# Decoding attention on one core: q spread two tiles ahead, and eight rows of the last V tile added beside the sum over groups

## Chip, cores, metric

One core of a Trainium2 chip. The metric is the device time of one launch in microseconds. The changed kernel and the kernel before are run in turn on the same chip.

## The reference

```python
B, H, Sq, Skv, Dh = 8, 32, 1, 4096, 128          # bfloat16
scores = einsum('bhqd,bhkd->bhqk', q, k) * Dh ** -0.5
out = einsum('bhqk,bhkd->bhqd', softmax(scores), v)
```

There is one query for each of the 256 heads. K and V are 268 MB each and are read once.

## The kernel before

Heads are worked in 32 tiles of 8. A tile of K or V is 8.4 MB: 128 partitions (16 per head) with 256 rows of 128 numbers each. For each tile the vector engine multiplies K by q and folds it, the tensor engine sums over the head's width, the scalar engine takes the exponentials `w`, and the tensor engine multiplies them with V.

```python
def q_prep(t):                       # spreads the q of 8 heads over 128 partitions
    ... matmul (L164); activation -> qg (L168); matmul (L170); activation -> qb (L172)

cuts = { ...
    ("v", NT - 1): [C // 2, C // 4, C // 8, C // 16, C // 32, LAST, LAST],   # C = 256, LAST = 4
}

def scores_of(t, u):
    if u == 0:
        scs[t] = sc_pool.tile([P, C], F32, name="sc", tag="sc")      # two buffers
    made = nc.vector.tensor_reduce(out=scs[t][:, ...], in_=sums.pop((t, u))[:], ...)   # L217

def values_of(t, lo, hi):            # four rows of V in a matmul; four column groups of the array
    end = C if t < NT - 1 else C - LAST
    group = [0 if t == NT - 1 and C // 2 <= c0 < C // 2 + 3 * C // 16 else c0 // CB % TG
             for c0 in range(0, end, CB)]
    ... matmul into avs[t][group j]                                   # L316

def result_of(t):                    # [cut]
    if t == NT - 1:
        for i in range(LAST):        # the last rows go straight into the result
            nc.tensor.matmul(ops[n][:], lhsT=w_last[:, i, :],
                             rhs=loads["v", t][:, C - LAST + i, :], ...)      # L354
    for m in range(CB):              # the sum over groups, from its copy
        nc.tensor.matmul(ops[n][:], lhsT=pick[...], rhs=comb[0:e, m, :], ...)  # L360

# main (cut)
    q_prep(0)
    for t in range(NT):
        product(t, 0, Q); sum_over_d(t, 0); ...
        if t + 1 < NT: q_prep(t + 1)
        ...
    values_of(NT - 1, 0, C // 2); norm_of(NQ - 1); recip_of(NQ - 1)
    values_of(NT - 1, C // 2, C - LAST)
    copy_of(NT - 1)                  # scalar engine: av -> comb, L344
    result_of(NT - 1); finish_of(NQ - 1); store_of(NQ - 1)
```

## Time and profile before

| | kernel before |
|---|---|
| timed runs | 1253.0, 1253.07, 1253.38 us |
| the profiled run | 1253.7 us, span 1251.9 us |
| HBM read | 536.94 MB, 429 GB/s over the span |
| DMA queue of K, V and q | 99.3% of 16 engines |
| vector, tensor, scalar engine busy | 83%, 61%, 14% |

The queue that carries K and V takes 99.3% of the DMA engines' time, so the end is set by when the last bytes of V land and by what stands behind them. The prediction below reads that tail.

The queues of the page, with packets, MB and share of 16 engines, show also the transfers that bring the instructions:

```profile
q1 hardware_dynamic: 11216, 536.94, 99.3%
q8 instruction: 14, 0.23, 0.1%
q14 instruction: 11, 0.09, 0.0%
```

They are small, 16 KB (q8) each, and take 0.93 to 1.10 us (q8) each in the trace, but the page counts their time as a share of the same 16 engines.

### The profile page before, as it was taken

Reading aid. Unit: us, or ns where it says so; the run is one execution under the profiler, and the core shown is the slowest. Engines: PE = TensorE matmul, PEld = TensorE weight load, DVE = VectorE, ACT = ScalarE, POOL = GpSimd, SP = SyncE. Lnnn points to the kernel's source line nnn. Section 1 sums busy time; section 2 is a strip of 40 time slices with the busy share of each in tenths; the row PEclk is TensorE's granted clock in tenths of the full one; section 3 lists DMA queues with packets and bytes.
Section 4 is the critical chain, followed back from the end, with each engine's and each line's share of the span. In section 5 each row is a group of like instructions: output and inputs, shape, how many; then the busy total and the mean of one; then the engine's idle time right before and its main releaser. Section 6 shows DMA issues by size and latency. Waiting matters only on the chain. (4 is left out here: it accounts for less than half of the span.)

```text
span 1251.9 us, 11042 instructions
## 1 busy us (share of the span) xinstructions
PE 767.1 (61%) x3075; PEld 286.0 (23%) x3075; DVE 1036.0 (83%) x586; ACT 170.6 (14%) x625; POOL 3.3 (0%) x18
## 2 busy tenths in 40 slices
PE   2465467755577555775557755577655676557856
PEld 0122122221222112222212221122211222212212
DVE  7887988888988889888798888987889888898792
ACT  0111011111011110111101111011110111101111
POOL 0000000000000000000000000000000000000000
PEclk8677788777887777887788877788777887779867
DMA  9999999999999999999999999999999999999997
GB/s 404 436 436 434 436 433 432 436 436 434 425 430 430 436 433 436 429 434 430 436 436 434 436 434 432 436 432 430 431 436 434 436 426 436 427 428 429 428 437 317
DMA packets 11577, 537.33 MB, mean 429 GB/s; under 512 B 1824, under 2 KB 2080, under 8 KB 2336
## 3 DMA queue, kind: packets, MB, share of 16 engines
q1 hardware_dynamic: 11216, 536.94, 99.3%
q8 instruction: 14, 0.23, 0.1%
q10 hardware_dynamic: 336, 0.07, 0.0%
q14 instruction: 11, 0.09, 0.0%
HBM read 536.94 MB, written 0.07 MB: 429 GB/s over the span
## 5 line engine op out<-in xcount | busy, mean ns | idle before, releaser
L185 DVE TENSOR_TENSOR kt<-kt,qb 128x8192 bf16<-128x8192 bf16 x128 | 565.3, 4416 | 127.2 <-DMA kt<-in_k_dram 98.9
L205 PE MATMUL ps<-kt,ident 128*128 128x512 bf16 x800 | 262.6, 479 | 434.3 <-DVE kt L193 368.3
L288 PE MATMUL av<-vt,w 128*32 x1740 | 424.5, 394 | 5.5
L188 DVE TENSOR_TENSOR kt<-kt 128x4096 bf16<-128x4096 bf16 x128 | 293.4, 2292 | 4.4
L288 PEld LDWEIGHTS av<-vt,w 128*32 x1740 | 171.9, 99 | 263.8 <-issue 124.9
L205 PEld LDWEIGHTS <-ident 128*128 128x128 bf16 x800 | 86.1, 112 | 597.2 <-issue 549.7
L249 ACT ACTIVATE w<-sc,bias 128x256 bf16<-128x256 f32 x256 | 126.3, 494 | 667.1 <-DVE bias L240 667.1
L217 DVE TENSOR_REDUCE sc<-ps 128x64 f32<-128x512 f32 x128 | 87.8, 686 | 56.6 <-PE ps L205 56.6
L193 DVE TENSOR_TENSOR kt<-kt 128x2048 bf16<-128x2048 bf16 x56 | 68.6, 1225 | 1.9
L344 ACT ACTIVATE comb<-av 32x512 bf16<-32x512 f32 (+1 forms) x32 | 18.7, 585 | 324.5 <-PEq L278 314.0
L274 PE MATMUL av<-vt,w 128*32 128x512 bf16 x116 | 47.1, 499 | 14.7 <-issue 13.2
L249 ACT ACTIVATION_READ_ACCUMULATOR w<-sc,bias 128x1 f32 x256 | 47.7, 186 | 0.0
L274 PEld LDWEIGHTS av<-vt,w 128*32 128x32 bf16 x116 | 6.9, 100 | 55.3 <-issue 55.3
L168 ACT ACTIVATE qg<-qh 8x128 bf16<-8x128 f32 x32 | 8.5, 266 | 76.5 <-PE qh L164 76.5
L316 PE MATMUL av<-vt,w 128*32 128x512 bf16 x191 | 16.4, 428 | 2.0 <-DMA vt<-in_v_dram 2.0
L360 PE MATMUL op<-comb,pick 32*16 32x128 bf16 (+1 forms) x128 | 12.3, 215 | 5.8 <-ACT comb L344 5.8
L229 DVE TENSOR_REDUCE pmax<-sc 128x1 f32<-128x256 f32 x32 | 13.5, 420 | 1.1
L170 PE MATMUL qp<-qg,heads 8*128 8x128 bf16 x32 | 6.9, 214 | 11.4 <-ACT qg L168 11.4
L164 PE MATMUL qh<-q_all,ident 128*8 128x128 bf16 x32 | 7.2, 224 | 8.4 <-DMA q_all<-in_q_dram 8.4
L172 ACT ACTIVATE qb<-qp 128x128 bf16<-128x128 f32 x32 | 8.9, 277 | 9.6 <-PE qp L170 9.6
L360 PEld LDWEIGHTS <-pick 32*16 32x16 bf16 (+1 forms) x128 | 6.8, 84 | 13.1 <-issue 12.7
L316 PEld LDWEIGHTS <-w 128*32 128x32 bf16 x191 | 6.8, 105 | 11.0 <-issue 7.2
(29 smaller groups left out, 46.7 us busy)
## 6 DMA issues: line engine op xcount, KB each, us to landing
kt<-in_k_dram SPq DMA_DIRECT2D x6, 4096.0 KB, 24.6
kt<-in_k_dram SPq DMA_DIRECT2D x4, 2048.0 KB, 13.9
vt<-in_v_dram SPq DMA_DIRECT2D x1, 4096.0 KB, 36.2
vt<-in_v_dram SPq DMA_DIRECT2D x1, 2048.0 KB, 40.8
vt<-in_v_dram SPq DMA_DIRECT2D x1, 1024.0 KB, 42.8
vt<-in_v_dram SPq DMA_DIRECT2D x1, 512.0 KB, 43.6
vt<-in_v_dram SPq DMA_DIRECT2D x31, 25.6
kt<-in_k_dram SPq DMA_DIRECT2D x28, 28.1
```

Source lines behind the costliest of these rows:

```text
L185: nc.vector.tensor_tensor(out=part, in0=part, in1=qb[:].to_broadcast([P, MC, D]), op=ALU.mult)
L188: nc.vector.tensor_tensor(out=part[:, :, 0 : D // 2], in0=part[:, :, 0 : D // 2], in1=part[:, :, D // 2 : D], op=ALU.add,)
L193: nc.vector.tensor_tensor(out=part[:, :, 0 : D // 4], in0=part[:, :, 0 : D // 4], in1=part[:, :, D // 4 : D // 2], op=ALU.add,)
L205: nc.tensor.matmul(ps[:], lhsT=ident[:], rhs=kt[:, u * UC : (u + 1) * UC, s * DS : (s + 1) * DS], start=(s == 0), stop=(s == n - 1),)
L217: made = nc.vector.tensor_reduce(out=scs[t][:, u * UC : (u + 1) * UC], in_=sums.pop((t, u))[:], axis=AX.X, op=ALU.add)
L229: nc.vector.tensor_reduce(out=pmax[:], in_=sc[:], axis=AX.X, op=ALU.max)
L249: nc.scalar.activation(out=w[:, :, g, :], in_=sc_g, func=ACT.Exp, bias=bias[:, g : g + 1], scale=scale, accum_out=esum[:, t % R, g : g + 1],)
L274: pe.matmul(av, lhsT=wf[:, i * nw : (i + 1) * nw], rhs=vf[:, i * nv : (i + 1) * nv], **how)
L288: pe.matmul(av, lhsT=wf[:, bass.ds(ow + i * nw, nw)], rhs=vf[:, bass.ds(ov + i * nv, nv)], start=False, stop=False,)
L316: nc.tensor.matmul(avs[t][j * AG : (j + 1) * AG, :], lhsT=w[:, i, :, :], rhs=vt[:, c0 : c0 + CB, :], start=(i < TG), stop=(j not in group[ ...
L344: nc.scalar.activation(out=comb[0:n, :, :], in_=av[0:n, :, :], func=ACT.Copy)
L360: nc.tensor.matmul(ops[n][:], lhsT=pick[0:e, m, r, :], rhs=comb[0:e, m, :], start=(r == 0 and m == 0), stop=(r == R - 1 and m == CB - 1),)
```

## The change

The intent as it reads: have each q ready earlier, and take one more matmul out of the chain behind the last landing, by adding eight rows and not four straight into the result.

```diff
-LAST = 4
+LAST = 8
-    q_pool = ... bufs=2
+    q_pool = ... bufs=3
-        ("v", NT - 1): [C // 2, C // 4, C // 8, C // 16, C // 32, LAST, LAST],
+        ("v", NT - 1): [C // 2, C // 4, C // 8, C // 16, C // 32, LAST // 2, LAST // 2],
-            nc.gpsimd.tensor_copy(... w_last ..., in_=w[:, (C - LAST) // CB, :, :])
+            for i in range(LAST // CB):
+                nc.gpsimd.tensor_copy(... w_last part i ..., in_=w[:, (C - LAST) // CB + i, :, :])
         q_prep(0)
+        q_prep(1)
         for t in range(NT):
             ...
-            if t + 1 < NT:
-                q_prep(t + 1)
+            if t + 2 < NT:
+                q_prep(t + 2)
```

The pieces of V keep their sizes (4 and 4 at the end).

## The prediction

Its sum: 0.0 for q and 0.0 to -0.05 us for the eight rows, on 1253.07, came to 1253.0. One more instruction block: that added instructions could need one, and the 1254 if one comes, are estimates. "Such blocks" in it are the 16 KB transfers of q8, and "cold" is half clock, at which the long matmuls of the first profile start 0.427 us apart and not 0.216.

> **What bounds the kernel now.** I read the summary page first, its slices of the span. The DMA row is at 9 in every slice but the last, while the vector engine stays at 7 to 9 and the tensor engine at 4 to 7.

> ```profile
> DVE  7887988888988889888798888987889888898792
> PEclk8677788777887777887788877788777887779867
> DMA  9999999999999999999999999999999999999997
> GB/s 404 436 436 434 436 433 432 436 436 434 425 430 430 436 433 436 429 434 430 436 436 434 436 434 432 436 432 430 431 436 434 436 426 436 427 428 429 428 437 317
> ```

> Added up over 20 us stretches, the DMA packets in the trace keep all 16 engines busy (mean 16.0) from about 5 us to 1240 us. So K and V set the pace: 536.94 MB at 433 GB/s, the usual rate of the slices, is 1240 us, and the measured span is 1251.9 us. The 12 us between are the ramp at the start, the uneven finish of the engines and the work behind the last bytes. Only the last of these has a part of the change in it.

> Next the timeline of the vector engine at the start of a tile, because the page blames several of its waits on the scalar engine, and the spread of q is made there.

> ```profile
> 81.04 4.43 DVE L185 TENSOR_TENSOR kt<-kt,qb 128x8192 bf16<-128x8192 bf16 x1 [3.73 <-DMA kt<-in_k_dram]
> 160.01 4.43 DVE L185 TENSOR_TENSOR kt<-kt,qb 128x8192 bf16<-128x8192 bf16 x1 [4.32 <-ACT stage L369]
> ```

> The second looks like a wait for the scalar engine. But the K tile landed at 159.82, and in the first case at 80.95: both products start 0.1 to 0.2 us after the landing. The same holds at every tile from 81 to 1091 us where this product stood waiting over 1 us. The name in brackets is a guess; the wait is for K.

> Last the chain that ended last, and the timeline of the tensor and scalar engines under it.

> ```profile
> 1201.69 40.81 DMA vt<-in_v_dram
> 1242.50 0.04 issue
> 1242.54 5.49 PE av L316 x29
> ...
> 1248.11 0.60 ACT comb L344
> 1248.72 0.04 issue
> 1248.76 0.40 PE op L360 x4
> 1249.15 0.02 issue
> 1249.18 0.36 ACT stage L369
> ```

> ```profile
> 1242.54 5.43 PE L316 MATMUL av<-vt,w 128*32 128x512 bf16 x31 [2.01 <-DMA vt<-in_v_dram]
> 1247.81 0.39 PE L354 MATMUL op<-vt,w_last 128*16 128x128 bf16 x4
> 1248.76 0.38 PE L360 MATMUL op<-comb,pick 128*16 128x128 bf16 x4 [0.56 <-ACT comb L344]
> ```

> V's last tile comes in seven pieces of 128, 64, 32, 16, 8, 4 and 4 rows. The chain names one landing only: that of the 64 rows at 1242.50. Then the tensor engine runs without a gap through its 31 matmuls to about 1248.0. The later pieces landed, by the transfers' own records, at 1244.99, 1246.21, 1246.86 (8 rows), 1247.20 (4 rows) and 1247.51 (last 4).

> What keeps it busy is column group 0. The kernel puts the first twelve matmuls of this stretch there, one after the other, and every fourth of the others: 17 in all. In the single records they start at 1242.54 and then 0.427 us apart, up to about 1245.87 (eight intervals with the first a little shorter), then 0.216 us apart; the last, of row 240, starts at 1247.592 and ends at 1247.97. The last matmul in program order, of rows 248 to 251, sits in group 2, started at 1247.24 just behind its landing, and is done before that. It is the one that the change removes.

> [...] the granted clock goes from half to full at 1245.81, one window after the boundary at 1242.40. [...] the best slices show 434 to 437[...]. [...] the page of the kernel before shows 14 such blocks (0.23 MB on q8). In the landings one engine is 1.4 us behind the next at the end, and it was 0.02 us behind before the first such block at 97 us. So added instructions could cost DMA time, if they need another block.

> **The change part by part.**

> *q two tiles ahead.* 32 spreads before and 32 after. Each is two matmuls (224 and 214 ns), two scalar activations (266 and 277 ns) and the handshakes: at 19.91 to 21.06 us it takes 1.15 us. In the order of instructions the second spread moves to the head, right behind the first; each later one takes the old place of the spread before it, and the last body that had one, at tile 30, has none. At the head the vector engine starts at 9.61 on the first q. The second spread comes behind that on both engines, about 9.6 to 10.8, where the tensor engine stands idle until 16.41 and the scalar engine until 20.22. Cost 0. In the loop no product waits for q, so gain 0. At tile 30 the tensor engine has about 1.1 us less to do, but the weights of tile 31 are ready at 1236.8, and from 1240.5 to 1242.54 the engine only waits for V: up to 2 us of such gain vanish there. The third buffers of qg and qb are 256 bytes per partition each. Sum: 0.

> *Eight rows straight into the result.* Removed: one 128x512 matmul, the one in group 2 that was not the last to end. Group 0's chain is the same 17 matmuls from the same landing. What may go is its completion: the semaphore that frees the scalar copy counts at 1247.993 and then 1248.027, so an estimate of 0.03 us. Added: four 128x128 matmuls, eight in place of four. The first started at 1247.81, 0.216 us behind the last long one, and they follow at 0.056 us: starts to 1248.20, end at 1248.20 + 0.22 = 1248.42. The copy of the sum runs from 1248.11 to 1248.71 beside them, and the four L360 matmuls that need it start at 1248.76. So 0.34 us of slack is left: cost 0. Their second four need the landing of 1247.51, past by then. The second POOL copy of weights is another 0.32 us behind 1237.39, ten us before its use. The larger memset (128x128 instead of 128x64; one of that size takes 0.19 us) lies at 2 us, before anything needs it.

> The pieces of V keep their sizes, so the transfers are the same. Sum of both: 0.0 to -0.05 us on 1253.07, so 1253.0.

> **The rivals.**

> *The landing of rows 248 to 251 was the real last wait.* Then the copy could start one landing earlier, 1247.20 - 1246.86 = 0.34 us: 1252.7. For it: it seems to be what the change is for. Against it: 1247.20 + 0.04 + 0.38 = 1247.62 is 0.35 us ahead of group 0's end. I give it one chance in five, in runs where the window of the clock falls better.

> *q held up the vector engine.* The rows that name the scalar engine before L185 add up to 17.4 + 4.2 us. If they were real, and if the vector engine set the end, the time would be about 1232. The landings contradict the first and the saturated DMA the second. One in a hundred.

> *The eight short matmuls outlast the copy.* [...]

> *The window of the clock falls elsewhere.* [...] In the profiled run it began 0.14 us before the landing, near the best case. At worst all 17 matmuls of group 0 are cold: nine more times 0.211 = 1.9 us, 1255. That is chance and not the change, and the three runs of before lie within 0.38 us.

> *One more instruction block.* The change adds three pairs of weight load and matmul to the tensor engine, six rows in 3030, and one instruction to POOL. [...] one DMA engine gets up to 1.1 us more (a block's time in the trace): 1254. Some 3 chances in 100.

> **Range and chances.** Point 1253.0. Downward the rival of the landing (0.34) and a spread like that of before (0.4) give 1252.3; upward the same spread and a window somewhat worse give 1253.8. A change of 2% is 25 us; that needs something in the DMA stream, which the change does not touch. Faster 0.01, same 0.985, slower 0.005.

> **What would show it.** Right: DMA at 9 throughout, the last landings near 1247.5, the copy of the sum about 0.6 us behind them, the eight short matmuls done before it, L185 still starting 0.1 us behind each K landing. The first step fails if the copy starts over 0.2 us earlier relative to the landing of the 64 rows; the second if the L360 matmuls start later than the copy's end; the part on q if L185 starts earlier relative to K's landing. The whole is wrong if the landings themselves shift, by instruction blocks on another engine or by a DMA queue that ran dry.

## The result, and the profile after

The changed kernel took 1252.65, 1252.72, 1252.76 and 1252.91 us, median 1252.74, against 1253.04 for the kernel before in four runs. The ratio is 0.9997 (95% interval 0.998 to 1.0014): no change at the 2% level. Ratios here are the mean time of one kernel's runs over that of the other's of the same rounds, so not quite the ratio of the medians. The time lies inside the predicted range. The profile shows another tail than the one predicted.

Slices of the span in the kernel after, in tenths for the granted clock and the DMA share:

```profile
PEclk9977788777887778877778777788777887778867
DMA  9999999999999999999999999999999999999997
```

The stream is as full as before. Its chain that ended last, in the same columns as before:

```profile
1204.53 41.99 DMA vt<-in_v_dram
1246.53 0.04 issue
1246.57 0.41 PE av L317 x2
...
1247.06 0.61 ACT comb L345
1247.66 0.04 issue
1247.71 0.40 PE op L361 x4
1248.10 0.02 issue
1248.13 0.36 ACT stage L370
```

And its tensor engine in the timeline:

```profile
1242.24 3.40 PE L317 MATMUL av<-vt,w 128*32 128x512 bf16 x24 [1.09 <-DMA vt<-in_v_dram]
1245.97 0.40 PE L317 MATMUL av<-vt,w 128*32 128x512 bf16 x4 [0.33 <-DMA vt<-in_v_dram]
1246.57 0.39 PE L317 MATMUL av<-vt,w 128*32 128x512 bf16 x2 [0.20 <-DMA vt<-in_v_dram]
1246.89 0.70 PE L355 MATMUL op<-vt,w_last 128*16 128x128 bf16 x8
```

In the kernel before the chain hung on the landing of the 64 rows at 1242.50 and was tensor work from there on. Here the tensor engine waits three times, and the chain hangs on the landing of the 8-row piece at 1246.53: two matmuls, the copy, the sum, the store. Its clock was full (granted 1.0 from 1233.70 to 1250.77 us; column group 0 advances by 0.216 us from the start), so group 0 was done early. The copy starts at 1247.06 and not at 1248.11. The two profiled runs, of 1253.7 and 1252.65 us, differ by as much as these two copies, 1.05 us. But the medians of the timed runs differ by only 0.3 us. So either the kernel before is not usually as its first profile shows it, or something was lost elsewhere.

The DVE (vector engine) timeline has one more difference. The first product of tile 29, in the kernel after and in the kernel before:

```profile
1091.92 4.43 DVE L185 TENSOR_TENSOR kt<-kt,qb 128x8192 bf16<-128x8192 bf16 x1 [4.25 <-DMA kt<-in_k_dram]
```

```profile
1091.27 4.43 DVE L185 TENSOR_TENSOR kt<-kt,qb 128x8192 bf16<-128x8192 bf16 x1 [4.25 <-DMA kt<-in_k_dram]
```

It is 0.65 us later. From there on the vector engine never waits for K again, and the last weights are later too: the last exponentials start at 1237.65 in place of 1236.34.

### The profile page after: what moved, and what is told of

It is laid out like the page before. It is cut to its first block, busy times and chain, and to the rows that moved or that the text cites. A ratio compares the mean times of both kernels' runs of the same rounds, so it can differ in the third digit from the quotient of the medians.

```text
span 1250.9 us, 11080 instructions
## 1 busy us (share of the span) xinstructions
PE 770.4 (62%) x3078; PEld 289.4 (23%) x3078; DVE 1036.1 (83%) x586; ACT 170.7 (14%) x625; POOL 3.5 (0%) x19
## 2 busy tenths in 40 slices
DMA  9999999999999999999999999999999999999997
## 3 DMA queue, kind: packets, MB, share of 16 engines
q1 hardware_dynamic: 11216, 536.94, 99.4%
HBM read 536.94 MB, written 0.07 MB: 429 GB/s over the span
## 5 line engine op out<-in xcount | busy, mean ns | idle before, releaser
L185 DVE TENSOR_TENSOR kt<-kt,qb 128x8192 bf16<-128x8192 bf16 x128 | 565.3, 4416 | 127.9 <-DMA kt<-in_k_dram 103.5
L205 PE MATMUL ps<-kt,ident 128*128 128x512 bf16 x800 | 265.3, 483 | 432.4 <-DVE kt L193 366.8
L217 DVE TENSOR_REDUCE sc<-ps 128x64 f32<-128x512 f32 x128 | 87.8, 686 | 57.3 <-PE ps L205 57.3
```

The costliest lines, as they stand in the source:

```text
L185: nc.vector.tensor_tensor(out=part, in0=part, in1=qb[:].to_broadcast([P, MC, D]), op=ALU.mult)
L205: nc.tensor.matmul(ps[:], lhsT=ident[:], rhs=kt[:, u * UC : (u + 1) * UC, s * DS : (s + 1) * DS], start=(s == 0), stop=(s == n - 1),)
L217: made = nc.vector.tensor_reduce(out=scs[t][:, u * UC : (u + 1) * UC], in_=sums.pop((t, u))[:], axis=AX.X, op=ALU.add)
```

## The experiments

"Slow tail" below means a time above 1253.3 us. This cut was set by hand: six of the 36 runs of the kernel before lie between 1253.26 and 1253.38, it is the same for kernels whose fast tails differ, and the tail itself was seen only in the profiled runs. The theories: **A**, in most runs the clock is full in the tail and the last wait is the landing of the piece ahead of the last one; **B**, group 0 on the half clock sets the end, as predicted; **C**, the gain is q's; **D** and its sharper forms **E** and **F** say that q acts on how often the clock is halved.

### The kernel before, unchanged

> The kernel before, unchanged: how far two builds of one thing differ, and whether its tail always looks as in the first profile (first matmul of the last 31 followed by others 0.427 us apart, no wait for the later pieces of V, copy of the sum at 1248.1). Theory A (in most runs the clock is full there and the last wait is for the landing of rows 248 to 251; the first profile, at 1253.7 the slowest of its four, caught a half clock): 1253.0 to 1253.1, and this profile, if it is near 1253.0, shows the matmuls 0.216 us apart and a wait for V just before the copy. Theory B (group 0's chain on the half clock sets the end in every run, as predicted): the same time, and the profile looks like the first.

Measured: 1252.98, 1253.03, 1253.04, 1253.35, 1253.58. The nine runs of the shared control beside it went from 1253.0 to 1253.9, three of them above 1253.3. Its profile is of the run of 1252.98:

```profile
1242.21 3.40 PE L316 MATMUL av<-vt,w 128*32 128x512 bf16 x24 [2.17 <-DMA vt<-in_v_dram]
1245.93 0.40 PE L316 MATMUL av<-vt,w 128*32 128x512 bf16 x4 [0.32 <-DMA vt<-in_v_dram]
1246.58 0.72 PE L316 MATMUL av<-vt,w 128*32 128x512 bf16 x3 [0.25 <-DMA vt<-in_v_dram]
1247.24 0.38 PE L354 MATMUL op<-vt,w_last 128*16 128x128 bf16 x4
1248.04 0.38 PE L360 MATMUL op<-comb,pick 128*16 128x128 bf16 x4 [0.42 <-ACT comb L344]
```

That is theory A's tail: full clock (granted 1.00 from 1236 to 1248 us), waits for each piece. The third group here holds three matmuls where the kernel after has two. The third is of rows 248 to 251, which landed at 1246.88 against 1246.54 for the 8-row piece, and the copy starts at 1247.39. The difference, 0.34 us, is what the change removes. One kernel has two tails. The profile that the prediction read was of a slow one.

### q alone

```diff
-LAST = 8
+LAST = 4          # and with it the old cuts and copy; q stays two tiles ahead
```

> Only q two tiles ahead. Theory A: 0.0 (ratio 1.000, within 0.1 us of the kernel before). Rival C (the 0.3 us come from q: less work of the tensor engine at tile 30, or another clock in the tail by it): -0.3 us.

Measured: 1252.98, 1253.03, 1253.04, 1253.15, 1253.49; ratio 0.9999. Its fast tail is that of the kernel before to 0.1 us. C as stated falls: q takes nothing from the fast tail. One run of the five, 1253.49, is above the cut.

### Eight rows alone

```diff
-        q_prep(1)
-            if t + 2 < NT:
-                q_prep(t + 2)
+            if t + 1 < NT:
+                q_prep(t + 1)
```

> Only the eight rows. Theory A: the copy waits for the 8-row piece in place of the 4-row piece behind it, 0.3 us earlier: -0.3 us against the kernel before (1252.7). Theory B: 0.0 to -0.05. Rival C: 0.0.

Measured: 1252.65, 1252.74, 1253.48, 1253.51, 1253.63. Two runs are at A's 1252.7, three at B's time. The profile is of 1253.63. Timeline of the tensor engine, and busy time by stretches (the two numbers before the last are the granted clock and the DMA share):

```profile
1242.42 5.52 PE L317 MATMUL av<-vt,w 128*32 128x512 bf16 x30 [2.17 <-DMA vt<-in_v_dram]
1247.77 0.61 PE L355 MATMUL op<-vt,w_last 128*16 128x128 bf16 x8
1248.69 0.38 PE L361 MATMUL op<-comb,pick 128*16 128x128 bf16 x4 [0.31 <-ACT comb L345]
```

```profile
1242.00:1244.00 2.00, 1.58 (x7) 0.69 (x7) 0.00 (x0) 0.00 (x0) 0.00 (x0) 0.86 0.89 347
1244.00:1246.00 2.00, 2.00 (x12) 0.70 (x11) 0.00 (x0) 0.00 (x0) 0.00 (x0) 0.50 0.36 133
```

The clock was halved at 1243.46, behind an idle stretch of 2.17 us, and came back at 1246.87. The 30 matmuls then run without a wait to 1247.9, past every landing that they need (1246.74 at the latest), and taking one matmul out of group 2 gains nothing: B holds in this tail. So the eight rows are worth 0.35 us in the fast tail (1252.70 against 1253.05, medians of the runs below 1253.3) and nothing to speak of in the slow one. But three of the five runs are slow, and none of the four of the whole change was: something else in it may prevent that.

### The kernel before with the clock held up

```diff
+    def fill(n):                       # nobody reads it
+        ps = ps_s.tile([P, UC, DS], F32, name="ps", tag="ps")
+        for i in range(n):
+            nc.tensor.matmul(ps[:], lhsT=ident[:], rhs=loads["k", NT - 1][:, 0:UC, 0:DS], ...)
                 values_of(t - 1, 0, C)
+                if t == NT - 1: fill(10)
 ...
         recip_of(NQ - 1)
+        fill(8)
         values_of(NT - 1, C // 2, C - LAST)
```

> The kernel before with 18 matmuls that nobody reads (10 behind the last matmuls of tile 30, 8 ahead of the wait for the 64 rows), so that the clock is full in the tail whatever its window. Theory A: as the kernel before, within 0.1 us (1253.0), and the profile shows the wait for the 4-row piece, about 0.03 us after its landing, then 0.38 us of matmul, then the copy. Theory B: the half clock costs 0.4 us or more in every run, so this is 0.4 us faster than the kernel before.

Measured: 1252.99 to 1253.29, median 1253.22, none slow. In its profile the first 24 of the last matmuls take 3.40 us, as at full clock in `before_again`. The copy starts at 1247.51, behind the landing of the 4-row piece at 1247.00, as A has it. The median is 0.17 us above the fast runs without the unread matmuls (1253.05), a little more than the 0.1 us that A allowed. B's 0.4 us of gain is not there. No run is above the cut of 1253.3, though three of the five are within 0.1 us of it.

### The changed kernel again

> The changed kernel again. So far its four runs all had the fast tail (1252.65 to 1252.91), the eight rows alone only two of five (1252.65 and 1252.74, the others 1253.48 to 1253.63), and q alone four of five. Theory D (spreading q earlier delays the last weights by a microsecond, which shortens the idle time of the tensor engine before the 64 rows, and so the half clock comes less often): at most one of five above 1253.3. Rival (the window's chance alone): one to three of five above 1253.3.

Measured: 1252.57 to 1252.82, none slow; with the first four runs, none of nine. Of the nine controls beside it five were slow. The kernel before was slow in 16 of 36 runs, with a mean of 1253.34; the changed kernel has a mean of 1252.71. Theory D's count came true, its reason did not: in this run's profile the half clock was there, from 1238.81 to 1242.22, and it ended as the 64 rows began (1242.16).

### The changed kernel with the clock held up

The edit is the same `fill`.

> The changed kernel with the same 18 unread matmuls. Theory A: no run above 1253.3, and 0.33 us faster than the kernel before with the unread matmuls (whose median was 1253.22): 1252.7 to 1252.9. Its profile shows the copy behind the landing of the 8-row piece. Theory B is out by the profiles of the first four.

Measured: 1252.65 to 1253.1, median 1252.70, none slow, ratio 0.9995. The same 24 matmuls take 3.41 us. The copy (1247.12) follows the landing of the 8-row piece (1246.59). Against the kernel before with the same edit this is 0.5 us by the medians, of two different calls; 0.33 was expected, and the copies in the two profiles are 0.39 us apart.

### Eight rows alone with the clock held up

> Eight rows, q one tile ahead, and the 18 unread matmuls that keep the tensor engine's clock up. Theory E (q's only worth is that its tail meets the half clock less often): no run above 1253.3, median within 0.15 us of the changed kernel with the same unread matmuls (1252.70). Rival (q is worth something on its own, or harms): off by more than that.

Measured: 1252.66 to 1252.86, median 1252.83, none slow; the 24 matmuls take 3.40 us. This is 0.13 us from the changed kernel with the clock held, within what was stated. So with the clock held, moving q is worth about nothing. Without, none of the nine runs with q moved was slow, and three of the five with the eight rows alone.

### Why moving q changes the clock

The traces suggest a link. The vector engine's instructions at L217, in the kernel after, by count and times in ns:

```profile
L217 DVE TENSOR_REDUCE sc<-ps x128: 682/684/693, 22.9 to 1232.2; 128x64 f32<-128x512 f32 x128
L217 DVEq EVENT_SEMAPHORE  x30: 21/21/21, 94.1 to 1211.7; - x30
```

The second row is absent in the kernel before. There the vector engine's wait for q of this tile also told it that the exponentials ahead of that q on the scalar engine had been read from `sc`, whose buffer it was about to write again. With q spread a tile earlier the wait for it comes before those exponentials, and the scheduler adds a wait of its own, 30 here and one at the reciprocal. They take 21 ns each, and the engine's idle time just ahead of L217's work is 57.3 us in all, against 56.6 before. But they are 31 more instructions, and the q14 instruction block that came at 1095.5 us comes at 1032.3 (the last one is then that of 1067.6, which stays in its place). In all four profiles with q two tiles ahead one DMA engine is then 1.3 to 1.7 us behind the next when the K tile of tile 29 lands (1091.74 to 1091.85); in the eight with q one tile ahead and nothing else added to the vector engine it is 0.4 to 0.8 us behind, and the landing is at 1090.83 to 1091.27. This K tile was issued at 1062.8 to 1063.3 in all of them, so it did not start later. That the moved block is what lays the engine behind is argued and not isolated: the block itself takes only 0.32 us. Beside it stands what the first block of q8 (0.93 us long, at 97.5 us) came with: in the first profile one engine was 0.02 us behind the next at the landing of 80.95 us and 1.34 us at that of 101.73; in the kernel after, 0.21 and 1.25 us. The next two runs try the two ends of this.

```diff
 def scores_of(t, u):                   # the eight rows alone, with 31 more vector instructions
+        if u == 0 and t > 0:
+            nc.vector.memset(pad[:], 0.0)        # one element
```

> Eight rows, q one tile ahead, and 31 vector memsets of one element, one for each tile but the first: as many added vector instructions as the 31 waits that moving q brought. Theory F (the added instructions bring the vector engine's last instruction block from 1095 to 1032 us, that lays one DMA engine behind by about 1 us when the K tile of 1091 lands, the last weights come later, the gap ahead of the 64 rows shrinks to 1 us, and the clock stays full): block at 1032, that K landing at 1091.7 to 1091.9 in place of 1090.8 to 1091.2, at most one of five above 1253.3. Rival (it is the place of q's matmuls and activations): block and landing as the eight rows alone, or three of five above 1253.3 in spite of them.

Measured: the block at 1017.9 (earlier than expected), the K landing at 1091.95, all five runs 1252.66 to 1252.80. The times are as F has it: q is where it was in the kernel before, and they are those of the changed kernel. But the clock did not stay full, as F said. It was half from 1240.40 to 1243.81, into the 30 matmuls that start with the 64 rows:

```profile
1239.33 2.57 PE L320 MATMUL av<-vt,w 128*32 128x512 bf16 x29
1242.35 4.76 PE L320 MATMUL av<-vt,w 128*32 128x512 bf16 x30 [0.42 <-DMA vt<-in_v_dram]
```

It came back early enough for these matmuls to catch up: the copy starts at 1247.21, 0.54 us behind the landing of the 8-row piece (1246.67), against 0.53 us in the kernel after.

```diff
 def weights_of(t):                     # the eight rows alone, with the vector engine held up
+        if t == NT - 2:
+            for i in range(2):
+                late = small.tile([P, 1], F32, name="late", tag="late")
+                nc.vector.tensor_reduce(out=late[:], in_=sc[:], axis=AX.X, op=ALU.max)
```

> Eight rows, q one tile ahead, and the vector engine held up by two reductions (0.84 us) nobody reads, in tile 30, behind every wait for K. Theory F: block at 1095 and K landing at 1091.0 as before, but the last weights 0.8 us later, the gap ahead of the 64 rows about 1.2 us in place of 2.0 to 2.2, and at most one of five above 1253.3; so work added to the vector engine makes the kernel's median faster, 1252.7. Rival: two to four of five above 1253.3, as the eight rows alone (three of five).

Measured: the block at 1095.3, the K landing at 1090.90, all five runs 1252.63 to 1253.01. Its tensor engine:

```profile
1238.60 3.52 PE L321 MATMUL av<-vt,w 128*32 128x512 bf16 x29
1242.31 3.40 PE L321 MATMUL av<-vt,w 128*32 128x512 bf16 x24 [0.16 <-DMA vt<-in_v_dram]
```

The gap ahead of the 64 rows is 0.16 us here and not 2.17, or the 1.2 that F expected, and the last exponentials start at 1237.02, 0.27 us later than with the eight rows alone (1236.75) and not 0.8. In this run the clock was half from 1238.7 to 1242.1, but the work on the first 128 rows then filled that time, and it was full again from 1242.1. So a delay of under a microsecond, on an engine that is not the bound, goes with the eight rows paying in all five runs. Together: with late weights (q alone, the changed kernel, and these two) 1 slow run of 24; with early ones and no unread matmuls (kernel before, eight rows, the two kernels of sixteen rows below) 22 of 51. The eight rows alone ran on another chip than the last two, but of the nine controls beside those two five were slow.

So in these profiles the clock went with the work in a window and not with the length of a gap, and where the window's ends fell made the difference. With early weights the window over the gap of 2.2 us held 1.24 us of matmuls in the profile of the eight rows alone (1240.05 to 1243.46: the clock fell) and 1.53 us in `before_again` (1240.33 to 1243.74: it stayed). In the first profile the clock had fallen at 1238.99, the next window held 1.54 us, with the gap in it, and the half clock went on to 1245.81. With late weights that next window held 3.0 to 3.4 us, because the first 128 rows fill it, and the clock was back at 1242.12 to 1243.81.

### Sixteen rows straight into the result

```diff
-LAST = 8
+LAST = 16          # q one tile ahead
-    ("v", NT - 1): [..., C // 32, LAST // 2, LAST // 2],
+    ("v", NT - 1): [..., C // 32, CB, CB],
```

> Sixteen rows straight into the result (pieces of V as before, q one tile ahead). Theory A: the copy then follows the landing of rows 224 to 239 (1245.9), is done by 1247.05, and the end follows the landing of the last piece (1247.2): its four matmuls, then the four that add the sum over groups, the last starting near 1247.63; against the changed kernel another 0.2 us: 1252.45 in runs with full clock. Rival (sixteen short matmuls are too long for the copy): no gain or a loss, 1252.7 or more.

Measured: 1252.42, 1252.46, 1252.52, 1252.60, 1253.12. The copy is at 1246.54 to 1247.14, and the end is the tensor engine's own string of short matmuls, in its chain:

```profile
1246.68 1.05 PE op L355 x16
1247.73 0.24 PE op L361 x4
1247.97 0.02 issue
1247.99 0.36 ACT stage L370
```

The median is 0.12 us below the changed kernel's 1252.64 (0.22 below its first median of 1252.74); A had 0.2. It was not repeated. The run of 1253.12 is below the cut, but 0.5 us above the other four.

### The same, with the sum added before the last four rows

```diff
-  rows 240..255 direct; then the sum over groups (pick x comb)
+  rows 240..251 direct; then the sum over groups; then rows 252..255 direct
```

> As last16, with the sum over groups added before the last four rows instead of behind them. Theory A: nothing but the last piece's four matmuls is left behind its landing: another 0.15 to 0.2 us, 1252.3 in runs with full clock. Rival: as last16, because the copy, not the landing, is the last wait.

Measured: 1252.72, 1253.0, 1253.55, 1253.64, 1253.77; the profiled run has the slow tail. Inconclusive by itself, so the clock was held up:

> Sixteen rows, the sum added before the last four, and the 18 unread matmuls. Theory A: no run above 1253.3; the end follows the landing of the last piece by four short matmuls: 1252.3, 0.35 us faster than the changed kernel. Rival: the twelve direct matmuls, or the copy, take the place of the landing: 1252.5 as last16 with full clock.

Measured: 1252.55, 1252.71, 1252.86, 1253.19, 1253.5; so the expectation of 1252.3 and of no run above 1253.3 failed. But the two slowest runs did not have a slow tail. Each run's record also gives the span from the first to the last instruction: in every other run of the experiments the time is 1.73 to 1.86 us above it, in the runs of 1253.5 and 1253.19 it is 2.80 and 2.69 us above, and 1.91 in that of 1252.71. Their spans, 1250.7 and 1250.5 us, are no longer than those of `last16` (median 1250.7). What was added lies outside the span; why is open. In the profile, of 1252.86, the clock is full (the first 24 of the last matmuls in 3.40 us), and the last landing was 1247.64 (1247.14 to 1247.51 in the other kernels):

```profile
1247.01 0.83 PE op L356 x12
1247.84 0.22 PE op L370 x4
1248.07 0.24 PE op L356 x4
```

From the 8-row landing the 20 short matmuls stand behind each other, and the store follows the last landing by 0.69 us, as in the kernel without the new order. Their sum is the bound, not their order, and the median span of 1250.8 us shows no gain over `last16`: the rival was right. Why V landed 0.3 us later here, one profile can't tell.

## Why the prediction was right, and where not

- **The time.** 1253.0 was predicted, 1252.74 measured, in the range of 1252.3 to 1253.8. No 2% was in reach: the stream of K and V is untouched and still full.
- **What bounds the kernel.** Right for the stream. Wrong for the tail: "What keeps it busy is column group 0" is true of the profile that it read, and by the cut on the time of 16 in 36 runs. In the others, as far as `before_again` stands for them, the last wait is for the landing of rows 248 to 251. The sign was on the table: 1253.7 in the profiled run, 1253.0 to 1253.38 in the timed ones. Two of its own signs of being wrong came: the copy starts 4.86 us behind the landing of the 64 rows in place of 5.61, and a K landing shifts, by 0.65 us.
- **Eight rows, "an estimate of 0.03 us".** This is the term that was mis-sized: it is 0.35 us in the fast tail (0.33 by the two copies, 1247.39 and 1247.06), and about zero in the slow. The rival named for it ("the landing of rows 248 to 251 was the real last wait") had the right 0.34 us, but got one chance in five, because the half clock was taken for the rule and not the accident.
- **Eight short matmuls beside the copy, cost 0.** Right: in the kernel after they run from 1246.89 to 1247.59, the copy to 1247.66.
- **q, "Sum: 0".** Right for its direct worth: 0.0 alone. Its sum of waits that name the scalar engine, 17.4 + 4.2 us, left out a row of 6.7 us for `qb`; that one is the wait at the head, for the first q. But it looked at the instructions for their order only. It counted no added instruction on the vector engine; the trace has 31 added waits, and with them an instruction block comes 63 us earlier and a landing and the last weights later. With 31 other added instructions the same came; that the block is the link stays argued. The prediction looked for added blocks (there is none: 14 on q8 and 11 on q14 before and after); it did not look for moved ones, though its last sentence names a shift of landings by instruction blocks on another engine.
- **The clock's window.** Named as chance, with "worst 1.9 us", and its place in the profiled run called "near the best case"; in `before_again` the clock is full all through the tail (1.00 from 1236 to 1248 us). The slow tail cost 0.3 to 0.9 us in 16 of 36 runs before, and it is not chance alone: with the change it came in none of nine.
- **The point.** That 1252.74 lies so near 1253.0 is in part luck: the prediction's tail is the slow one and its gain near zero, while its 1253.0 was taken from timed runs that mostly had the fast one, where the gain is 0.35.

## What to carry to other kernels

Compare the time of the profiled run with the timed ones before reading its tail; where they differ by more than the change is worth, the profile may show the other of two tails. The chain of tensor work behind a landing had two limits here, its own length at the clock it got (copy at 1248.11, the clock half until 1245.81) and the next landing (copy at 1247.39, the clock full); which one held went with the work in the clock's window ahead of it (1.54 us in a window at half clock left it half, 1.53 us in one at full clock left it full). Moving q earlier added 31 waits that were implied before, so compare the waits and not only the order.
